# Attention and two-expert routing in one Trainium2 kernel: product banks kept from attention, the last batch's gate logits planned in attention, a third staging buffer

## The chip, the cores and the metric

One core of one Trainium2 chip runs the whole program in one launch. The metric is the device time of that launch in microseconds (us), taken on the chip. The kernel before has a median of 739.53 us over three runs (738.2 to 739.78). Five engines work side by side: PE (matrix products; its weight loads are listed as PEld), DVE and ACT (elementwise work), POOL (elementwise work and indirect transfers), and SP, whose queue only issues transfers.

## The reference, cut to what matters

Attention with 4 sink columns and a window of 128, then a mixture of 8 experts with the two best experts of each row:

```
q, k, v: (4 batches, 8 heads, 768 rows, 64)        # x: 3072 rows of 512
scores = where(sink | in_window, q @ k.T / 8, -1e9)
a = softmax(scores);  x = a @ v                    # heads side by side
noisy = x @ w_gate + log1p(exp(x @ w_noise)) * noise
top2 = the two best experts of a row; weights = softmax over the two
out[row] = sum over its two experts of weight * (relu(x @ w1[e]) @ w2[e])
```

## The kernel before, in words

The program has two parts, and each is first recorded and then laid out by a planner (class `Plan`). Every operation is recorded with its engine, a duration, a priority and what it reads and writes; `Plan.run` then lists the operations engine by engine, taking the ready one with the smallest priority, and issues the instructions in that order. Engines work their lists strictly in order, so the planner's durations and latencies decide only the order, through what counts as ready. The priorities come from the tables `PR`, `BY` and `P2`, which are the same before and after.

The first part is attention (`attention`). Its unit is a block n of 256 query rows of a pair of heads; a batch has 4 pairs of 3 blocks, so there are 48 blocks. A block has a score side: two products into the score banks `S` (L400), the previous window copied by ACT (`prev`, L404), the current window copied under a mask by DVE (`cur`, L409 and L411), the row maximum on DVE (`mins`, L421), the subtraction on POOL (`sub`), the exponential on ACT (`exps`), and for two blocks at once the row sums on DVE (`sums`, L431, and their reciprocal, L442). Up to 6 blocks may be in flight on that side (ring `C`). Behind it lies the value side: transposes of the probabilities into bank `P` (L463), copied by ACT (`CT`) and masked (`CM`); a small transpose (`pct`, L458) whose copy feeds the sink products (`sinks`, L501); the products with the values into a bank `X` (`pv`, L485 and L488); ACT's copy of the result into `turned` (L510); two transposes back (`rows`, L515); and the scaled result into `strip`, from where it is stored to `x_rows` in DRAM.

When all four pairs of a batch are there, `logits` makes the gate logits of 256 rows: products with the gate weights (`proj`, L710), ACT's copy, two transposes (`turn`, L718), and on DVE a scaling and a sum (`scale`, `total`). `routing` turns a batch's logits into places: the two best experts, the ranks (L824 to L830), and the product that puts each row number into its slot, here called the place product (`place`, L911, from the operands `rt_op` and `rt_tc`). Batches 0 to 2 are routed inside the first part. The first four tiles of 128 rows of expert 0 come from them alone: they are gathered by POOL (L1015), transposed by PE (L1099) and split by ACT and DVE into a high and a low part in `xe` (L1108 and L304).

The second part begins with these four tiles: products into the banks `H` (L1318 to L1320) and `Y` (L1350 to L1352). The last batch's logits and its routing are recorded in this part and lie between those products. Then the rows of experts 1 to 7 are gathered by POOL into a staging buffer `sg` (L1030), stored sorted to DRAM and loaded again (`xg`), and each expert's products follow (L1455 to L1457 and L1486). An output tile is scaled by ACT (L1359) into one of three `y` buffers and added into the output by POOL (L1374).

PSUM has eight banks. Attention uses four for `S`, one for `P` and three for `X`; the second part opens its own pool and takes two for `H`, one for `X`, one for `TX` and four for `Y`.

Of the kernel before, what the change touches and what calls it, by code (L numbers as in the profile page):

```python
# [75 lines left out]
SWITCH = {1: .06, 2: .05}  # L76


class Plan:
# [62 lines left out]
    def dma(self, prio, fn, us, r=(), w=(), u=(), n=1, late=0):  # L142
        self.count["dma"] = d = self.count.get("dma", -1) + 1
        self.op("SP", .48 * n, prio, fn, r, list(w) + [("dma", d)], u, lat=.65)
        self.op("DMA", us, prio, None, list(r) + [("dma", d)], w, u, lat=.95 + late)

    def run(self, dry=False):
# [21 lines left out]
        for _ in range(n):  # L169
# [26 lines left out]
            for s in succ[i]:  # L196
# [3 lines left out]
                if lat is None:  # L200
                    lat = (0 if e == "PE" else .06) if e == self.ops[s][0] else self.LAT.get((e, self.ops[s][0]), .2)
# [105 lines left out]
def attention(tc, plan, consts, cst, sh, qk_t, v, vsink, xbuf):  # L307
# [7 lines left out]
                      CT=2, CM=2, ps=2, xr=3, S=2, P=PB, X=XB, xtn=5, lt=1, lm=1, lg=2)  # L315
# [223 lines left out]
    def pair(m):  # L539
# [8 lines left out]
        op("PE", .27, n + .6 + P(g, "sinks"), lambda: sinks(m), r=[("ps", m), ("vr", (n - 1) // NJ // HP), ("vr", g // HP)], w=both, kind=3)  # L548

    def behind(n):  # L550
# [7 lines left out]
        op("ACT" if by else "DVE", .56 if by else .34, n + .7 + P(g, "rows_c"), lambda n=n, f=rows_by if by else rows_c: f(n),  # L558
# [17 lines left out]
    for g in range(NP):  # L576
        p0 = g * NJ
        e = p0 - NJ
        if g:
            load(g, None, ((g - 3) * NJ + PR.get("load_qk", 0) if g > 1 else -1980) + BY.get("load_qk", ZERO)[g])  # L580
            loads_v(g)
        else:
            plan.dma(-1997, lambda: load_v(0), 1.9, w=[("vn", 0)])
        if g % HP == 0:
            b, z = g // HP, (g - HP) * NJ if g else -6
            plan.dma((z if g else -1996.5) + BY.get("load_st", ZERO)[g], lambda b=b: sink_values(b), 2.2, w=[("st", vst[b])])
# [7 lines left out]
        for jj in range(NJ):  # L594
# [23 lines left out]
            op("PE", .44, n + .5 + P(g, "ptr"), lambda n=n: ptr(n), r=[("C", n)], w=[("P", n + NJ)], lat=(0, .21))  # L618
# [76 lines left out]
def logits(nc, plan, cst, sh, b, jj, z):  # L695
# [4 lines left out]
    last = b == sh.B - 1  # L700
    tag = "TX" if last and jj % 2 else "X"
# [23 lines left out]
    def total():  # L725
        nc.vector.tensor_reduce(get("lg", b, [128, NT, 2 * E])[:, 2 * jj:2 * jj + 2, :],
                                get(*mk).rearrange("p t h e -> p t e h"), op=OP.add, axis=AX.X)

    region = [("old", 0)] if last else []
# [7 lines left out]
def routing(nc, plan, cst, sh, b, t0, nt, z, xbuf):  # L737
# [72 lines left out]
    dve(topi, ["no", "mx"], ["ix"], .125 * nt)  # L810
# [60 lines left out]
    if not last:  # L871
        dve(lambda: v.tensor_scalar(rt("pp", pair, I32), rt("g"), 127, None, op0=OP.bitwise_and), ["g"], ["pp"], .08)
    dve(lambda: v.tensor_scalar(rt("tq", pair, I32), rt("g"), 7, None, op0=OP.logical_shift_right), ["g"], ["tq"], .08)
    if last:
        dve(lambda: v.scalar_tensor_tensor(rt("pp", pair), rt("tq"), -128.0, rt("g"), op0=OP.mult, op1=OP.add), ["g", "tq"], ["pp"], .08)
# [3 lines left out]
    def rows_of(k):  # L879
        o = rt(f"op{k}", [128, nt, 128], F16)  # L880
        for i in range(nt):
            v.tensor_scalar(o[:, i, :], c["io"], rt("pp")[:, k, i:i + 1], None, op0=OP.is_equal)

    def cols_of(k):
        o = rt(f"tc{k}", [128, nt, E * TE], F16)
        for i in range(nt):
            v.tensor_scalar(o[:, i, :], c["io1"], rt("tv")[:, k, i:i + 1], c["tok"][:, T0 + i:T0 + i + 1], op0=OP.is_equal, op1=OP.mult)

    wide = [128, nt, E * TE]
    for k in range(2) if not last else ():  # L890
# [115 lines left out]
def gather(plan, nc, cst, sh, xbuf, e, t, z, after=None):  # L1006
# [16 lines left out]
    rows, sg = cst["xsort"][m], ("sg", m + 5)  # L1023
# [22 lines left out]
    plan.op("Pool", P2["gather"], zs, sort, r=[("rt_idi", sh.B - 1)] + held, w=[sg], lat=P2["lands"])  # L1046
    plan.dma(zs, store, 1.6, r=[sg], w=[("xs", n)], late=P2["late"])
    plan.dma(z, load, 1.4, r=[("xs", n)], w=[row], late=2)
# [78 lines left out]
def w_chunk(plan, nc, cst, sh, w1, w2, e, m, i, z, lo_eng="DVE", first=()):  # L1127
# [27 lines left out]
    plan.dma(z, load, 2.2, r=list(first) + ([("at", e)] if e else []), w=[("st", n)], late=P2["late"] if e else 0)  # L1155
# [53 lines left out]
def rows_seven(plan, nc, sh, e, group, z):  # L1209
# [40 lines left out]
    split(0, 2, lambda: raw(0))  # L1250
    sums(lambda: extra(0, 2), lambda: raw(1, 2, 4), lambda: raw(1, 0, 2))
# [39 lines left out]
def experts(tc, plan, cst, sh, w1, w2, xbuf, out):  # L1291
# [9 lines left out]
    plan.rings.update(w1=4, w2a=2, w2b=2, x7=1, hb=1, ws=2, wc=2, wx=2, pick=2, raw=2, old=1, u=3, ext=2, h=FC + 1, y=3, H=2, Y=4, TX=1)  # L1301
# [9 lines left out]
    def up(q, f, i):  # L1311
        e, tiles, width = info[q]
        p = get("H", FC * q + f, [128, width], F32, "ps", [128, 512])
        both = halves(plan, sh, q)
        w = first_w(plan, f // 2).rearrange("p (x k f) -> p x k f", x=2, k=4)
        w = w[:, :, :, f % 2 * 128:(f % 2 + 1) * 128]
        xh, xl = (x[:, i, :width] for x in both)
        nc.tensor.matmul(p, w[:, 0, i], xh, start=(i == 0), stop=False)  # L1318
        nc.tensor.matmul(p, w[:, 0, i], xl, start=False, stop=False)
        nc.tensor.matmul(p, w[:, 1, i], xh, start=False, stop=(i == DC - 1))  # L1320

# [63 lines left out]
    def ends(e, t, n, z):  # L1385
# [8 lines left out]
        op("Pool", 2.65, z, lambda: scatter(e, t), r=[("y", n), ix] + [("zero", i) for i in zeros], w=[("o", n)], lat=3)  # L1394

    z = 0
    for q, (e, tiles, width) in enumerate(info):
# [14 lines left out]
        for f in range(FC):  # L1412
            k = FC * q + f
            zu = z + f * dz
            for i in range(DC):
                op("PE", (UP1 * width + .19) / DC, zu, lambda q=q, f=f, i=i: up(q, f, i),
                   r=[(x, e, t) for x in ("xh", "xl") for t in tiles] + [("w1", f // 2)], w=[("H", k)],
# [83 lines left out]
    for e in range(1, E):  # L1501
# [8 lines left out]
        for g, group in enumerate(groups):  # L1510
            for t in group:
                gather(plan, nc, c, sh, xbuf, e, t, z0 + P2["ga"] + P2["gs"] * t, begun(e, t))
                weight(plan, nc, c, sh, e, t, z0 + P2["wt"] + 3 * t)
            rows_seven(plan, nc, sh, e, group, z0 + P2["x"] + P2["xs"] * g)
# [131 lines left out]
def phase_one(tc, nc, plan, ac, tail, cst, sh, qk_t, v, vsink, w1, w2, xbuf, out):  # L1646
# [19 lines left out]
    for n in attention(tc, plan, ac, cst, sh, qk_t, v, vsink, xbuf):  # L1666
# [4 lines left out]
        if g % HP == HP - 1 and g < (sh.B - 1) * HP:  # L1671
            soon.append((n + 1, g // HP, jj))
    for t in range(sh.FA):
# [12 lines left out]

def lay_out(plan, sh, turned, of_pair, strip):
# [16 lines left out]
def carried(plan, sh):  # L1704
    n = sh.H // 2 * sh.S // 256
    return [(kx, plan.wrote[kx][-1]) for kx in (("xt", i) for i in range((sh.B - 1) * n, sh.B * n))]


def phase_two(tc, nc, plan, cst, sh, w1, w2, xbuf, out):
# [14 lines left out]
    for jj in range(NT // 2):  # L1724
        logits(nc, plan, cst, sh, b, jj, -200)
# [78 lines left out]
```

## Time and profile before

| what | us |
|---|---|
| median of three runs | 739.53 |
| profiled execution | 739.88 |
| its span, first to last instruction | 738.3 |
| PE busy | 700.4 (95%) |
| DVE busy | 546.5 (74%) |
| ACT busy | 409.1 (55%) |
| POOL busy | 324.5 (44%) |

The span is 1.58 us shorter than the execution it comes from. Shares of busy time are averages over stages that are limited by different engines, so the table alone does not say what a change is worth; the rows further down are taken by stage.

### The profile page before, as it was taken

To read this page: it belongs to the slowest core of one execution; us is meant where nothing else is said; L and a number is where in the kernel's file an instruction comes from. 1 tells how busy PE (TensorE), PEld (TensorE's weight loads), DVE (VectorE), ACT (ScalarE), POOL (GpSimd) and SP (SyncE) were. 2 spreads that over 40 slices of the span, in tenths; PEclk is the share of its full clock that TensorE was granted. 3 is DMA by queue.
4 is the path that set the end of the run, shared out by engine and by line. 5 is a ranking of instruction groups with operands and counts; after the bars stand their busy time and mean duration, and the time that the engine had idled before them with its cause. 6 is when DMAs were issued, how large, how long until landed. Compare 5 with 4: busy or idle time off the path is not lost.

```text
span 738.3 us, 13436 instructions
## 1 busy us (share of the span) xinstructions
PE 700.4 (95%) x4731; PEld 587.1 (80%) x4731; DVE 546.5 (74%) x1300; ACT 409.1 (55%) x924; POOL 324.5 (44%) x431
## 2 busy tenths in 40 slices
PE   5999998998999999998999999999999999999995
PEld 3666666666768989888888998899889889889984
DVE  6699999986753898694878678676877878775710
ACT  3877788685222465554664456455555546555520
POOL 4567698795332552283226223431632440080022
PEclk9999999999999999999999999999999999999998
DMA  8565786646267998767747663857485393263133
GB/s 302 149 201 156 219 266 185 214 124 187 69 203 223 239 274 255 220 150 172 210 121 183 164 190 83 210 156 206 93 227 174 94 214 104 87 115 86 58 44 44
DMA packets 87320, 123.13 MB, mean 167 GB/s; under 512 B 18641, under 2 KB 55377, under 8 KB 87249
## 3 DMA queue, kind: packets, MB, share of 16 engines
q1 hardware_dynamic: 75856, 94.64, 41.8%
q0 software_dynamic: 11392, 27.60, 19.6%
q8 instruction: 38, 0.62, 0.4%
q14 instruction: 34, 0.27, 0.1%
HBM read 81.49 MB, written 40.73 MB: 166 GB/s over the span
## 4 chain that ended last, share of the span: by engine, by line
PE 73%; DVE 9%; ACT 7%; DMA 6%; issue 2%; POOL 1%; SPq 0%; POOLq 0%; ACTq 0%; DVEq 0%
PE Y L1486 28%; PE H L1455 5%; PE H L1456 5%; PE H L1457 5%; PE X L1455 3%; PE X L1457 3%; PE X L1456 3%; PE S L400 2%; ACT strip L521 2%; DMA st<-in_w2c 2%; PE P L463 2%; DMA out<-tmp,idx 2%; PE Y L1489 2%; PE X L485 1%; PE H L1318 1%
## 5 line engine op out<-in xcount | busy, mean ns | idle before, releaser
L1374 POOL DMA_INDIRECT out<-tmp,idx x34 | 80.5, 2367 | 157.0 <-ACT tmp L1359 149.0
L1486 PE MATMUL Y<-w2a,hb 128*128 128x512 f32 x504 | 129.5, 396 | 0.0
L1486 PE MATMUL Y<-w2b,hb 128*128 128x512 f32 x504 | 124.5, 391 | 0.0
L1486 PEld LDWEIGHTS Y<-w2b,hb 128*128 128x128 f32 x504 | 94.5, 188 | 19.8
L1486 PEld LDWEIGHTS Y<-w2a,hb 128*128 128x128 f32 x504 | 94.5, 188 | 19.4
L1456 PE MATMUL H<-x,wr 128*128 128x384 f32 (+1 forms) x224 | 77.1, 344 | 0.3 <-DVE x L304 0.3
L1030 POOL DMA_INDIRECT sg<-x_rows,rt_idi x45 | 48.6, 1080 | 54.6 <-DMA x_sorted<-sg 32.1
L304 DVE TENSOR_TENSOR wr<-st,wr 128x512 fp32r<-128x512 f32 (+1 forms) x86 | 59.7, 697 | 9.0 <-ACT wr L1185 8.3
L1185 ACT ACTIVATE wr<-st 128x512 fp32r<-128x512 f32 x84 | 52.3, 625 | 17.7 <-DVE st L304 17.2
L1455 PE MATMUL H<-xe,wr 128*128 128x384 f32 (+1 forms) x168 | 58.2, 347 | 2.5 <-ACT tmp L1470 1.7
L304 POOL TENSOR_TENSOR cbuf<-cbuf,mn 128x528 f32<-128x528 f32 x48 | 52.5, 1096 | 11.9 <-DVE mn L421 7.3
L1457 PE MATMUL H<-xe,wr 128*128 128x384 f32 (+1 forms) x168 | 57.6, 343 | 0.0
L400 PE MATMUL S<-kq 64*64 64x196 f32 (+1 forms) x768 | 48.4, 354 | 7.7 <-DVE cbuf L411 5.0
L1374 POOL DMA_INDIRECT out<-turned,idx x18 | 36.2, 2012 | 36.5 <-ACT turned L1359 30.2
L1045 POOL COPY spacer<-hb 1x1 f32<-1x1 f32 x38 | 12.0, 315 | 89.0 <-ACT hb L1476 81.8
L1359 ACT ACTIVATE tmp<-Y,wc 128x512 f32<-128x512 f32 x31 | 21.3, 688 | 50.4 <-PE Y L1486 28.9
L1470 ACT ACTIVATE tmp<-H 128x384 f32<-128x384 f32 (+1 forms) x56 | 28.0, 500 | 34.1 <-PE H L1457 31.0
L1456 PEld LDWEIGHTS H<-x,wr 128*128 128x128 f32 x224 | 42.1, 188 | 2.8 <-DVE x L304 0.6
L411 DVE COPY_PREDICATED cbuf<-le,S 128x256 f32<-128x256 uint8 x80 | 33.8, 442 | 12.1 <-ACT cbuf L404 11.7
L400 PEld LDWEIGHTS S<-kq 64*64 64x64 f32 x768 | 22.6, 138 | 24.0 <-DVE cbuf L411 12.6
L304 DVE TENSOR_TENSOR w2a<-st,w2a 128x1024 fp32r<-128x1024 f32 x16 | 19.6, 1223 | 27.3 <-ACT w2a L1144 27.3
L1455 PE MATMUL X<-x,wr 128*128 128x384 f32 (+1 forms) x112 | 38.7, 345 | 1.1 <-ACT x L1241 1.1
(335 smaller groups left out, 1809.7 us busy)
## 6 DMA issues: line engine op xcount, KB each, us to landing
st<-in_w1c SPq DMA_DIRECT2D x32, 512.0 KB
st<-in_w2c SPq DMA_DIRECT2D x32, 512.0 KB
x_sorted<-sg SPq DMA_DIRECT2D x45, 272.0 KB
kq<-in_qk_t SPq DMA_DIRECT2D x15, 780.0 KB
xg<-x_sorted SPq DMA_DIRECT2D x42, 272.0 KB
out<-zt SPq DMA_DIRECT2D x31, 256.0 KB
vn<-in_v SPq DMA_DIRECT2D x16, 384.0 KB
x_rows<-strip SPq DMA_DIRECT2D x48, 128.0 KB
```

Of the source, the lines that this page charges most:

```text
L304: eng.tensor_tensor(out, a, b, op=OP.subtract)
L400: nc.tensor.matmul(whole[x, h, c0:c1], kq(g)[r, KS + 128 * j + 64 * s:KS + 128 * j + 64 * s + 64], kq(g)[r, o + c0:o + c1], start=True, st ...
L411: nc.vector.copy_predicated(c, le[:, None, :].to_broadcast([128, 2, 128]), p)
L1030: nc.gpsimd.indirect_dma_start(out=stage(), out_offset=None, in_=xbuf, in_offset=bass.IndirectOffsetOnAxis(ap=cst["idw"]()[:, sh.TE * e + ...
L1185: plan.op("ACT", .03 + .255 * m, z, lambda: nc.scalar.activation(h(), src(), AF.Copy), r=[st], w=[(*key, b)] + old, u=[key, ex], lat=P2["s ...
L1359: nc.scalar.activation(get("y", Y[e, t], [128, DM]), get("Y", Y[e, t]), AF.Copy, scale=c["wc"][e % 2][:, t:t + 1])
L1374: d = nc.gpsimd.indirect_dma_start(out=out, out_offset=bass.IndirectOffsetOnAxis(ap=c["idx"][:size(e, t), e, t:t + 1], axis=0), in_=get("y ...
L1455: nc.tensor.matmul(p, wh, h, start=start and not k, stop=False, skip_group_check=True)
L1456: nc.tensor.matmul(p, wh, l, start=False, stop=False, skip_group_check=True)
L1457: nc.tensor.matmul(p, wl, h, start=False, stop=k == 1, skip_group_check=True)
L1470: nc.scalar.activation(u_of(e, k), src(), AF.Copy)
L1486: nc.tensor.matmul(p, h[:, x * (CAP + R) + 128 * t:x * (CAP + R) + 128 * t + 128], w[:, y], start=(f == 0 and x + y == 0), stop=(f == FC - ...
```

## The change: what it does

1. The four banks of `P` and `X` are now four tiles `B0` to `B3` that outlive attention. In the second part `H`, `X` and `TX` are views of them; the pool of the second part holds `Y` alone.
2. The last batch's logits are recorded in the first part, each 256 rows after their last attention block, as for the other batches. The second part starts with the routing of that batch.
3. Sorted rows are staged in three buffers: every third tile goes to the end of `xe`, behind the split rows of the seven experts. The first use waits until the products that read `xe` whole are done.
4. The operands of the last batch's place product are made by whole-tile operations, as for the other batches, and not row by row.
5. The rows of expert 1 get other priorities.
6. The planner's costs change (same-engine latencies on DVE and ACT, changes of tile shape on PE, transfers). They cost nothing themselves, but move instructions.

```
-SWITCH = {1: .06, 2: .05}
+SWITCH = {1: .105, 2: .09}
+SELF = {"PE": 0, "DVE": .14, "ACT": .15}
...
-        self.op("DMA", us, prio, None, list(r) + [("dma", d)], w, u, lat=.95 + late)
+        self.op("DMA", us, prio, None, list(r) + [("dma", d)], w, u, lat=1.2 + (.6 if us > .7 else 0) + late)
...
-                    lat = (0 if e == "PE" else .06) if e == self.ops[s][0] else self.LAT.get((e, self.ops[s][0]), .2)
+                    lat = SELF.get(e, .06) if e == self.ops[s][0] else self.LAT.get((e, self.ops[s][0]), .2)
...
-    last = b == sh.B - 1
-    tag = "TX" if last and jj % 2 else "X"
+    tag = "X"
...
-    for k in range(2) if not last else ():
+    for k in range(2):
...
-    for k in range(2) if last else ():
-        dve(lambda k=k: rows_of(k), ["pp"], [f"op{k}"], .1 * nt, kind=PORT)
-        dve(lambda k=k: cols_of(k), ["tv"], [f"tc{k}"], .085 * nt, kind=PORT)
...
-    rows, sg = cst["xsort"][m], ("sg", m + 5)
+    rows = cst["xsort"][m]
+    sg = ("sx", m // 3) if m % 3 == 2 else ("sg", 5 + m // 3 * 2 + m % 3)
...
-    plan.op("Pool", P2["gather"], zs, sort, r=[("rt_idi", sh.B - 1)] + held, w=[sg], lat=P2["lands"])
+    plan.op("Pool", P2["gather"], zs, sort, r=[("rt_idi", sh.B - 1)] + held + [("xe", f) for f in range(sh.F // 128)] * (m == 2), w=[sg], lat=P2["lands"])
...
-            rows_seven(plan, nc, sh, e, group, z0 + P2["x"] + P2["xs"] * g)
+            rows_seven(plan, nc, sh, e, group, z0 + P2["x"] + (P2["xs"] if e > 1 else 5) * g, 20 if e == 1 else 0)
...
-            logits(nc, plan, cst, sh, b, jj, n + PR.get("lg", .5))
-            if jj == NJ - 1:
+            logits(nc, plan, cst, sh, b, jj, n + PR.get("lg" if b < sh.B - 1 else "ll", .5))
+            if jj == NJ - 1 and b < sh.B - 1:
...
-        if g % HP == HP - 1 and g < (sh.B - 1) * HP:
+        if g % HP == HP - 1:
...
+def banks(*regions):
+    held = {}
+
+    def get(i, shape, dt):
+        if shape is not None:
+            held[i] = view(regions[i % len(regions)], 0, shape, dt)
+        return held[i]
+
+    return get
...
-    for jj in range(NT // 2):
-        logits(nc, plan, cst, sh, b, jj, -200)
...
+            flat = both.enter_context(tc.tile_pool(name="flat", bufs=1, space=bass.MemoryType.PSUM))
+            bank = [flat.tile([128, 512], F32, name=f"B{i}") for i in range(4)]
...
+            plan.laid.update(P=banks(bank[0]), X=banks(*bank[1:]), xtn=of_pair, xr=lambda n, shape, dt: view(strip, n % 3 * 256, [128, 2, 2, sh.D], F32))
...
+        k = (plan.count["X"] + 1) % 3
+        near = [bank[1 + (k + i) % 3] for i in range(3)]
+        p2.laid.update(H=banks(near[0], bank[0]), X=banks(near[1]), TX=banks(near[2]))
```

DVE's list near the end of attention, before, from the last operand of batch 2's place product (`rt_tc1`) on; `cbuf` holds the score side, `mn` its maxima, `sm` its sums, and `idg` is the list by which expert 0's first rows are gathered:

```order
L895 TENSOR_TENSOR rt_tc1_2775<-io1_85,rt_tv_2754 128x336
L409 TENSOR_TENSOR cbuf_163<-S0_74,m0_160 128x2x128
L411 COPY_PREDICATED cbuf_163<-le_156,S1_75 128x2x128
L421 TENSOR_REDUCE mn_2800<-cbuf_163 128x4
L411 COPY_PREDICATED cbuf_163<-le_156,S0_74 128x2x128
L421 TENSOR_REDUCE mn_2833<-cbuf_163 128x4
L926 SCALAR_TENSOR_TENSOR idg_134<-X_2820,ga_111 128x4
L928 TENSOR_TENSOR idx_135<-X_2820,sa_112 128x4
L953 TENSOR_TENSOR ids_107<-ids_107,X_2820 128x56
L411 COPY_PREDICATED cbuf_163<-le_156,S0_74 128x2x128
L421 TENSOR_REDUCE mn_2861<-cbuf_163 128x4
L431 TENSOR_REDUCE sm_2875<-cbuf_163 128x8
```

The same place in the changed kernel's DVE list:

```order
L882 TENSOR_TENSOR rt_tc1_2753<-io1_92,rt_tv_2713 128x336
L432 TENSOR_REDUCE sm_2756<-cbuf_170 128x8
L443 RECIPROCAL ri_2191<-sm_2756 128x4x2
L525 TENSOR_TENSOR strip_151<-B1_75,ri_2191 128x256
L910 SCALAR_TENSOR_TENSOR idg_141<-B3_77,ga_118 128x4
L912 TENSOR_TENSOR idx_142<-B3_77,sa_119 128x4
L937 TENSOR_TENSOR ids_114<-ids_114,B3_77 128x56
L525 TENSOR_TENSOR strip_151<-B2_76,ri_2191 128x256
```

All masked copies and maxima of the score side now stand ahead of the place product's operands; behind them, one sum is left of two.

PE's list where attention ends and the first expert's products begin, before (`xe` are the four split tiles, `wr` the weights; `sg` and `xg` the gathered rows):

```order
L485 MATMUL X_2964<-CT_2979,vn_2857 64x128 x4
L488 MATMUL X_2964<-CM_2969,dv_2934 64x128 x4
L515 MATMUL X_2936<-idf_66,turned_143 128x128 x2
L1099 MATMUL X_3002<-idf_66,sg_2901 128x128 x4
L515 MATMUL X_2964<-idf_66,turned_143 128x128 x2
L1099 MATMUL X_3012<-idf_66,sg_2932 128x128 x4
L1099 MATMUL X_3021<-idf_66,xg_2961 128x128 x4
L1099 MATMUL X_3030<-idf_66,xg_2983 128x128 x4
L710 MATMUL X_3056<-turned_143,wbd_80 32x256 x4
L710 MATMUL TX_3061<-turned_143,wbd_80 32x256 x4
L1318 MATMUL H_3067<-xe_3010,wr_1588 128x512
```

And in the changed kernel:

```order
L489 MATMUL B1_75<-CM_2862,dv_2840 64x128 x4
L516 MATMUL B3_77<-idf_66,turned_150 128x128 x2
L710 MATMUL B2_76<-turned_150,wbd_87 32x256 x4
L516 MATMUL B1_75<-idf_66,turned_150 128x128 x2
L710 MATMUL B3_77<-turned_150,wbd_87 32x256 x4
L718 MATMUL B2_76<-idf_66,lt_2918 128x128 x2
L1093 MATMUL B1_75<-idf_66,sg_2811 128x128 x4
L718 MATMUL B3_77<-idf_66,lt_2935 128x128 x2
L1093 MATMUL B2_76<-idf_66,sg_2828 128x128 x4
L1093 MATMUL B1_75<-idf_66,xg_2857 128x128 x4
L1093 MATMUL B3_77<-idf_66,xg_2833 128x128 x4
L1066 MATMUL B2_76<-xe_2939,wr_1418 128x512
```

The logits' products and transposes (L710, L718) now stand among the last attention rows and the row tiles, and none is left among the expert's products.

## Rows read from the trace of the kernel before

**Rows 1.** The page: busy time, share of the span and instructions of each engine.

```profile
PE 700.4 (95%) x4731; PEld 587.1 (80%) x4731; DVE 546.5 (74%) x1300; ACT 409.1 (55%) x924; POOL 324.5 (44%) x431
```

**Rows 2.** Busy time by stretch: length, each engine, then granted clock, DMA share, GB/s.

```profile
10.00:60.00 50.00, 44.75 (x540) 31.26 (x536) 40.81 (x74) 37.95 (x109) 30.39 (x46) 0.97 0.61 196
60.00:163.00 103.00, 94.73 (x1304) 65.98 (x1303) 97.66 (x260) 83.52 (x253) 84.72 (x142) 1.00 0.70 203
183.00:214.00 31.00, 29.17 (x177) 21.80 (x178) 21.90 (x102) 8.28 (x15) 10.38 (x14) 1.00 0.43 129
214.00:331.00 117.00, 116.64 (x573) 102.18 (x572) 87.17 (x209) 56.33 (x112) 53.09 (x58) 1.00 0.81 224
331.00:353.00 22.00, 18.33 (x90) 16.36 (x89) 11.82 (x30) 9.79 (x20) 9.19 (x11) 1.00 0.75 174
353.00:704.00 351.00, 350.27 (x1725) 315.05 (x1724) 266.73 (x574) 192.81 (x370) 108.81 (x109) 1.00 0.56 145
```

**Rows 3.** DVE, 162 to 184 us, in order of time: start, us, what, idle before.

```profile
162.56 0.92 DVE L895 TENSOR_TENSOR rt_tc<-io,rt_tv 128x336 f16<-128x336 f16 x2
...
165.98 0.45 DVE L411 COPY_PREDICATED cbuf<-le,S 128x256 f32<-128x256 uint8 x1 [1.23 <-ACT cbuf L404]
166.46 0.70 DVE L421 TENSOR_REDUCE mn<-cbuf 128x4 f32<-128x528 f32 x1
...
168.65 1.25 DVE L431 TENSOR_REDUCE sm<-cbuf 128x8 f32<-128x1064 f32 x1
...
170.15 0.20 DVE L442 RECIPROCAL ri<-sm 128x8 f32<-128x8 f32 x1
...
181.68 1.34 DVE L304 TENSOR_TENSOR xe<-X,xe 128x512 fp32r<-128x512 f32 x2
```

**Rows 4.** PE, 164 to 191 us, in order of time.

```profile
165.39 0.61 PE L911 MATMUL X<-rt_tc,rt_op 128*128 128x56 f16 x12
...
170.52 0.44 PE L501 MATMUL X<-ps,vr 64*128 64x128 f32 x4
170.89 0.66 PE L485 MATMUL X<-CT,vn 128*64 128x128 f32 x8
171.38 0.61 PE L488 MATMUL X<-CM,dv 128*64 128x128 f32 x8
171.91 0.66 PE L463 MATMUL P<-idf,cbuf 128*128 128x128 f32 x4
...
172.68 0.44 PE L515 MATMUL X<-idf,turned 128*128 128x128 f32 x2
...
181.03 0.63 PE L1099 MATMUL X<-idf,xg 128*128 128x128 f32 x4 [0.25 <-DMA xg<-x_rows,idg]
183.07 0.64 PE L710 MATMUL X<-turned,wbd 128*32 128x256 f32 x8 [1.41 <-DVE xe L304]
...
184.88 0.38 PE L718 MATMUL X<-idf,turned 128*128 128x128 f32 x2
```

**Rows 5.** What PE waited for, 183 to 330 us: total us, times, longest.

```profile
PE TX L1099 <- DMA sg<-x_rows,idg: 0.9, 1, 0.9
PE X L824 <- DVE m L816: 0.4, 1, 0.4
PE X L948 <- DVE x L943: 0.4, 1, 0.4
```

**Rows 6.** Waits, 305 to 362 us, the rows of the output path.

```profile
ACT tmp L1359 <- DMA out<-tmp,idx: 8.6, 2, 6.8
...
POOL sg L1030 <- DMA x_sorted<-sg: 5.8, 2, 3.5
```

**Rows 7.** Stretches in which PE is little busy, columns as in rows 2.

```profile
24.00:26.00 2.00, 1.26 (x21) 0.83 (x20) 1.46 (x5) 2.00 (x6) 1.35 (x3) 1.00 0.80 162
...
28.00:30.00 2.00, 2.00 (x18) 1.11 (x15) 1.23 (x3) 1.25 (x4) 1.47 (x3) 0.50 0.60 188
...
178.00:184.00 6.00, 3.46 (x34) 2.03 (x32) 3.71 (x10) 2.78 (x6) 0.06 (x1) 1.00 0.82 192
```

More of the change, by code (lines that the diff above doesn't have):

```diff
@@ L870, in routing @@
         ["ix", "r2"], ["g"], .08)
-    if not last:
-        dve(lambda: v.tensor_scalar(rt("pp", pair, I32), rt("g"), 127, None, op0=OP.bitwise_and), ["g"], ["pp"], .08)
+    dve(lambda: v.tensor_scalar(rt("pp", pair, I32), rt("g"), 127, None, op0=OP.bitwise_and), ["g"], ["pp"], .08)
     dve(lambda: v.tensor_scalar(rt("tq", pair, I32), rt("g"), 7, None, op0=OP.logical_shift_right), ["g"], ["tq"], .08)
-    if last:
-        dve(lambda: v.scalar_tensor_tensor(rt("pp", pair), rt("tq"), -128.0, rt("g"), op0=OP.mult, op1=OP.add), ["g", "tq"], ["pp"], .08)
     dve(lambda: v.tensor_scalar(rt("vl", pair), rt("r2"), float(sh.CAP), None, op0=OP.is_lt), ["r2"], ["vl"], .08)
@@ L1074, in rows_region, with up_part @@
     return plan.get("hb", 0, [128, 8 * (2 * CAP + 64)], F32R, "sb")
+def up_part(plan, nc, sh, q, f, i, width, p):
+    w = first_w(plan, f // 2).rearrange("p (x k f) -> p x k f", x=2, k=4)[:, :, :, f % 2 * 128:(f % 2 + 1) * 128]
+    xh, xl = (x[:, i, :width] for x in halves(plan, sh, q))
+    nc.tensor.matmul(p, w[:, 0, i], xh, start=(i == 0), stop=False)
+    nc.tensor.matmul(p, w[:, 0, i], xl, start=False, stop=False)
+    nc.tensor.matmul(p, w[:, 1, i], xh, start=False, stop=(i == sh.DM // 128 - 1))
 def first_w(plan, i):
@@ L1154, in w_chunk @@
         plan.op("SP", .3, z - .01, which, r=[("eid", 0)], w=[("at", e)])
-    plan.dma(z, load, 2.2, r=list(first) + ([("at", e)] if e else []), w=[("st", n)], late=P2["late"] if e else 0)
+    plan.dma(z, load, 1.35, r=list(first) + ([("at", e)] if e else []), w=[("st", n)], late=P2["late"] if e else 0)
     if e and m == 1:
@@ L1250, in rows_seven @@
     split(0, 2, lambda: raw(0))
+    z += more
     sums(lambda: extra(0, 2), lambda: raw(1, 2, 4), lambda: raw(1, 0, 2))
@@ L1311, in up @@
     def up(q, f, i):
[L1312 to L1320, printed above, removed]
+        up_part(plan, nc, sh, q, f, i, info[q][2], get("H", FC * q + f, [128, info[q][2]], F32, "ps", [128, 512]))
     def cut(q):
@@ L1416, in experts @@
                 op("PE", (UP1 * width + .19) / DC, zu, lambda q=q, f=f, i=i: up(q, f, i),
-                   r=[(x, e, t) for x in ("xh", "xl") for t in tiles] + [("w1", f // 2)], w=[("H", k)],
+                   r=[(x, e, t) for x in ("xh", "xl") for t in tiles] + [("w1", f // 2)], w=[("H", k)] + [("xe", f)] * (not q),
                    u=region + [("wr", f // 2), ("hb", 0)])
@@ L1704, in carried @@
 def carried(plan, sh):
-    n = sh.H // 2 * sh.S // 256
-    return [(kx, plan.wrote[kx][-1]) for kx in (("xt", i) for i in range((sh.B - 1) * n, sh.B * n))]
+    return [(kx, plan.wrote[kx][-1]) for kx in [("lgs", (sh.B - 1) * sh.S // 256 + i) for i in range(sh.S // 256)]]
 def phase_two(tc, nc, plan, cst, sh, w1, w2, xbuf, out):
```

56 lines of the change are left out of this document (25 added, 31 removed).

## The prediction, made before the changed kernel ran

> **What bounds the kernel now.** I read four views in this order. First the stretches: PE is busy 116.64 of 117 us from 214 to 331 and 350.27 of 351 from 353 to 704, so with its 95% [rows 1, 2] the second part is a solid row of products. A delay of the first of them passes undiminished to the end. Only two places there are loose: 183 to 214 us, with 1.83 us idle, and 331 to 353, with 3.67 [rows 2]. Second, the same view for attention: from 60 to 163 us DVE is busy 97.66 of 103 us and PE 94.73 [rows 2]; from 10 to 60 DVE has 40.81 of 50. So DVE carries attention, with 9.19 + 5.34 = 14.5 us idle between 10 and 163. Third, the instructions where attention ends: batch 2's place product lies at 165.39 to 166.00, and everything of expert 0's start hangs on it: indices, gather, transposes on PE, splits on DVE. PE is let go by the last split at 183.07, runs two `proj` of the logits, and starts the first expert product at 184.07 [rows 3, 4]. Fourth, the waits of the second part [rows 5, 6].
>
> So the time is: the moment of the place product, plus 18.07 us to the first expert product, plus a nearly solid rest.
>
> **The change, term by term.** All sums are made on the profiled execution, 739.88 us (738.3 of span and 1.58 around it); the median of the runs is 0.35 lower, which I take off at the end.
>
> 1. *DVE ahead of the place product.* The order shows that after the change all masked copies and maxima stand ahead of the operand `rt_tc1`. Compared line by line over the whole of DVE's list up to there, that is four more current-window copies (I price the one L409 among them as an L411), three more maxima, one more sum and one more reciprocal: 4 x 0.45 + 3 x 0.70 + 1.25 + 0.20 = 5.35, taken as 5.3 us [rows 3]. Either they push the place product back by all of it, or they fill idle time that DVE had. With 14.5 us idle in 153, and the planner's costs for DVE now larger, so that it lists fewer steps behind one they depend on, about half should be filled: 2.5 us. Net +2.8. Bounds: nothing filled, +5.3; 8 us filled, a little over half of the idle time, -2.7. This is the least certain term, since an order shows no idle time.
>
> 2. *From the place product to the first expert product.* Before, 18.07 us. Behind the place product only four blocks remain after the change, not six, but the logits' work joins them. PE's share by rows: two sink products 2 x 0.44; four value products, each pair of L485 and L488 some 1.10 (170.89 to 171.99), 4.4; four row transposes 4 x 0.44, 1.76; two transposes into `P`, 2 x 0.66, 1.32; three `proj` at 0.5 (two fill 183.07 to 184.07), 1.5; three `turn` at 0.38, 1.14; four row tiles at 0.63, 2.5. Sum 13.5 us [rows 4]. The chain isn't gapless: results go PE to ACT to PE, PE to DVE to PE, some six times, and a step like the last wait of PE, 1.41 us, or the 0.25 for the gather, stands for each; at 0.7 that is 4.5. Then the last split of a pair, 1.34 [rows 3], with ACT's high part ahead of it, some 0.6: 20 us in all, against 18.07: +1.9. Bounds: 15.5 if the waits are only the last two (13.5 + 1.34 + some 0.6), which is -2.6; 21.5 if each wait is 1 us, +3.4.
>  The same place shows what is moved: on DVE the logits' scaling and sum now lie between the splits of the row tiles, on a queue that works strictly in order, so a late `turn` holds a split and the first product behind it. Before, they lay behind the splits.
>
> 3. *Logits among the products.* Before, the third `proj` and three `turn` sat between the products: 0.5 + 3 x 0.38 = 1.64 by adding [rows 4]. Matrix products overlap at their ends, so less than that goes; I take 1.2, with 0.8 and 1.64 as bounds. Saved: -1.2.
>
> 4. *Routing of the last batch.* Its logits are ready some microseconds earlier relative to the products, and its operands are made whole-tile, as the 0.92 us of L895 in batch 2 [rows 3], not row by row. PE waited 0.9 + 0.4 + 0.4 = 1.7 us in this stretch [rows 5]. I take 1.2 of these as saved; bounds -1.7 and 0. The gather wait of 0.9 can stay, as the list behind it still has to pass POOL and a transfer. Taken: -1.2.
>
> 5. *Expert 1.* In 331 to 353 us PE idles 3.67 [rows 2]; beside it ACT waited once 6.8 us for an output transfer and POOL up to 3.5 us for a sorted store [rows 6]. The third staging buffer takes that POOL wait away, and the sorted gather no longer lies among expert 1's output transfers in POOL's list. But ACT's wait is for a transfer out of a `y` buffer, and that is untouched. Taken: -0.5. Bounds: the whole gap, -3.7; or, where the third buffer's first gather, which now waits for all products that read `xe`, holds the gathers behind it, +3.
>
> 6. *At nothing.* The four PSUM banks add no instruction; their cover is that `H`, `X` and `TX` are views of banks whose last readers in attention end before the products start. Without it one reader, a row transpose's scaled copy, would hold the first product for one of the six waits of term 2, 0.7 us. The planner's costs take no time themselves; what they move is in terms 1 and 2. The ring `lg` of one serves three batches in turn, each read by routing long before the next is written, so it is hidden; a wait there would stand on DVE's `total`, and cost the same 0.7.
>
> Sum: 739.88 + 2.8 + 1.9 - 1.2 - 1.2 - 0.5 = 741.7; on the scale of the median 741.3.
>
> **The clock, weighed apart.** PE was busy 1.26 of 2 us from 24 to 26, and its granted clock stood at 0.50 from 28 to 30, the lower of the two levels, 1.2 GHz: 2 us there did the work of one. But from 178 to 184 PE was busy 3.46 of 6 and the clock stayed at 1.00 [rows 7]. So sparse stretches here can cost the clock or not, and the end of attention has kept it so far. The Trainium skill, "TensorE: Matmul & The Clock Gate", section "HAM oscillation — how this bites in real kernels", says that a stream of products which stalls between bursts is put back to half clock, and that each burst then starts cold. By that rule a thinner tail of attention would take time beyond term 2; the row at 24 us agrees with it, the row at 178 us doesn't. By the row alone, nothing is added; by the rule, at least the 1.0 us that the row at 28 us lost.
>
> **The rivals.**
> *A. The attention itself gets shorter.* If DVE's idle time is filled by 8 us and not by 2.5, term 1 becomes -2.7 and the sum 736.2, or 735.8 as a median. It ends on the faster side from 4.3 us filled on (741.7 less 1.8 is 739.9). For it: 9.19 us of idle lie in 10 to 60 us, where DVE is no bound at all and where an order with truer latencies has most to give. Against it: from 60 to 163 us it is at 95% already.
> *B. Expert 1 starts late.* The sorted gather into the end of `xe` holds POOL's list for the 3.5 us that its longest wait for a buffer had [rows 6], in place of -0.5: 741.7 + 4 = 745.7, 745.3 as a median. For it: one more condition on a queue in order. Against it: the products that read `xe` end long before experts 1 to 7 are wanted, and PE has no idle in 214 to 331.
> *C. The change doesn't do what it says.* The logits leave one full stretch of PE for another, and what attention gains it gives back at the place product: terms cancel, 739.5.
> *D. The clock falls in the thinner tail.* One or two such stretches of 2 us at half clock before the first product, at 1.0 us lost in each [rows 7]: 742.3 to 743.3.
>
> **How the numbers follow.** A difference of 0.2%, 1.5 us, is about what a measurement of this kernel can tell from no change: faster is below 738.05, slower above 741.0. The forecast has 0.42: its own range is 739.5 to 744, of which 0.31 lies above 741.0 and 0.11 within. A has 0.32, 0.30 of it faster and 0.02 within. B has 0.09 and D 0.05, all slower. C has 0.12: 0.05 faster, 0.06 within, 0.01 slower. Faster 0.35, same 0.19, slower 0.46. The range goes from 734.5, where A has filled some 9 us, to 747, where B comes on top of +1.7 from the other terms.
>
> **What would show it.** Term 1: the end of the place product, 166.0 before; I expect 168.8, A expects 163 or less. And DVE's idle time from 10 us to that product, about 12 against some 6. Term 2: from the end of the place product to the first expert product, 20 us. Term 3: no `proj` or `turn` among the products. Term 4: the waits of 1.7 us behind the first products down to some 0.5. Term 5: PE's idle time around the end of expert 0, 3.2 us; under B over 6, with POOL's wait for the row buffer in the stretch before. D: a granted clock below 1.00 in the 15 us before the first product. The forecast is wrong if the first expert product starts before 186 us, which needs either the place product earlier or the tail shorter.

## The result, and the profile after

The changed kernel takes 747.42 us (745.87 to 749.59, 4 runs) against 738.87 before (737.43 to 739.78, 4 runs). The ratio is 1.012 with a 95% interval of 1.0088 to 1.0151: slower by 8.6 us (1.2%). The forecast was 741.3, with a range up to 747. The profiled execution is the shortest of the four, 745.87 us, with a span of 744.2.

The busy time of each engine has hardly moved:

```profile
PE 704.3 (95%) x4731; PEld 588.0 (79%) x4731; DVE 548.4 (74%) x1282; ACT 409.9 (55%) x924; POOL 314.4 (42%) x431
```

The stretches of the changed kernel, with the columns and the bounds of [rows 2]:

```profile
10.00:60.00 50.00, 46.13 (x574) 31.24 (x574) 43.42 (x80) 38.93 (x113) 33.16 (x50) 1.00 0.65 218
60.00:163.00 103.00, 91.43 (x1187) 62.76 (x1186) 92.08 (x222) 79.18 (x233) 76.88 (x125) 0.93 0.61 182
183.00:214.00 31.00, 28.58 (x209) 21.56 (x210) 21.97 (x85) 10.92 (x22) 8.81 (x14) 1.00 0.46 131
214.00:331.00 117.00, 112.81 (x554) 97.75 (x553) 78.63 (x191) 52.32 (x105) 43.04 (x55) 1.00 0.78 225
331.00:353.00 22.00, 22.00 (x104) 19.17 (x103) 18.63 (x49) 10.97 (x25) 13.26 (x13) 1.00 0.89 191
353.00:704.00 351.00, 350.35 (x1727) 315.33 (x1726) 270.40 (x577) 193.60 (x372) 108.40 (x111) 1.00 0.56 148
```

Against [rows 2], 10 to 60 us has become better: DVE is busy 43.42 us and not 40.81. But from 60 to 163, DVE falls from 97.66 to 92.08, and the mean granted clock to 0.93. In the second part PE's gap at 331 to 353 is gone, and 4.19 us of idle time stand ahead of it, from 214 to 331, where there was 0.36.

Two instructions of PE give the sum: the place product of batch 2, and the first product of the experts. In the kernel before they are at 165.39 [rows 4] and here:

```profile
184.07 0.50 PE L1318 MATMUL H<-xe,wr 128*128 128x512 f32 x1
```

In the changed kernel:

```profile
177.04 0.47 PE L895 MATMUL B<-rt_tc,rt_op 128*128 128x56 f16 x12
...
193.74 0.50 PE L1066 MATMUL B<-xe,wr 128*128 128x512 f32 x1 [0.74 <-ACT xe L1102]
```

The place product ends at 177.51, 11.5 us later than the 166.0 of [rows 4]. From there to the first product it is 16.23 us and not 18.07: 1.84 less. From the first product to the end of the span it is 550.46 (744.2 - 193.74) and not 554.23 (738.3 - 184.07): 3.77 less. 11.5 - 1.84 - 3.77 = 5.9, the difference of the spans. So everything that was lost lies ahead of the place product. Up to there, from 10 us on, DVE (the third engine column) has done more work and has also been idle longer; the kernel before and then the changed one:

```profile
10.00:166.00 156.00, 142.34 (x1875) 99.30 (x1871) 140.24 (x337) 124.47 (x373) 118.12 (x194) 0.99 0.67 198
10.00:177.51 167.51, 150.35 (x1919) 103.60 (x1919) 147.99 (x345) 129.45 (x383) 123.09 (x200) 0.96 0.61 188
```

DVE's work is 7.75 us more (147.99 against 140.24), its idle time 3.76 us more (19.52 against 15.76); together they are the 11.5.

Where most of it arose, is seen from the finished blocks. ACT copies each block's result into `turned`; the 18th and the 19th copy stand so, in the kernel before:

```profile
81.32 0.37 ACT L510 ACTIVATE turned<-X 128x256 f32<-128x256 f32 x1
85.88 0.38 ACT L510 ACTIVATE turned<-X 128x256 f32<-128x256 f32 x1 [0.24 <-PE X L488]
```

and in the changed one:

```profile
76.07 0.38 ACT L511 ACTIVATE turned<-B 128x256 f32<-128x256 f32 x1
92.68 0.36 ACT L511 ACTIVATE turned<-B 128x256 f32<-128x256 f32 x1
```

The changed kernel is 5.3 us ahead after 18 blocks, and 6.8 behind after 19: it loses 12 us at one place. At the 36th block, the last of batch 2, it is still 6.7 us behind (149.91 against 143.20). The other 4.8 us come between that block and the place product: 27.60 us against 22.80, in which 8 more blocks are finished and not 6. The place of the 12 us in steps of 2 us (columns as in [rows 2]):

```profile
82.00:84.00 2.00, 0.55 (x9) 0.35 (x9) 2.00 (x6) 1.40 (x5) 2.00 (x3) 1.00 0.91 294
84.00:86.00 2.00, 1.02 (x24) 0.51 (x16) 2.00 (x6) 1.50 (x5) 1.25 (x3) 0.67 0.93 358
86.00:88.00 2.00, 2.00 (x24) 1.12 (x16) 2.00 (x4) 1.31 (x3) 1.12 (x2) 0.50 1.08 375
88.00:90.00 2.00, 0.10 (x2) 0.00 (x0) 2.00 (x4) 0.09 (x1) 0.54 (x2) 0.50 0.91 353
90.00:92.00 2.00, 1.45 (x14) 1.45 (x16) 0.50 (x1) 0.82 (x1) 1.42 (x1) 0.50 0.39 149
92.00:94.00 2.00, 1.86 (x14) 1.26 (x11) 0.12 (x1) 1.80 (x5) 1.68 (x1) 0.50 0.04 18
94.00:96.00 2.00, 2.00 (x16) 1.47 (x14) 1.08 (x4) 0.88 (x2) 1.72 (x4) 0.77 0.22 66
```

DVE works without a break to 90 us, while PE starves; then PE runs at half clock, and DVE has nothing to do. What DVE did and what PE wanted, in order of time:

```profile
87.02 0.82 DVE L305 TENSOR_TENSOR dv<-vn 128x640 f32<-128x640 f32 x1
87.75 0.21 DVE L443 RECIPROCAL ri<-sm 128x8 f32<-128x8 f32 x1
87.87 1.22 DVE L432 TENSOR_REDUCE sm<-cbuf 128x8 f32<-128x1064 f32 x1
89.01 0.69 DVE L422 TENSOR_REDUCE mn<-cbuf 128x4 f32<-128x528 f32 x1
89.62 0.20 DVE L443 RECIPROCAL ri<-sm 128x8 f32<-128x8 f32 x1
89.73 0.77 DVE L305 TENSOR_TENSOR dv<-vn 128x640 f32<-128x640 f32 x1
93.88 0.42 DVE L525 TENSOR_TENSOR strip<-B,ri 128x256 f32<-128x256 f32 x1 [3.38 <-ACT turned L511]
```
```profile
86.98 1.12 PE L486 MATMUL B<-CT,vn 128*64 128x128 f32 x8
90.55 0.69 PE L489 MATMUL B<-CM,dv 128*64 128x128 f32 x4 [2.45 <-DVE dv L305]
```

PE holds the value product of head pair 6 and waits for that pair's `dv`, the difference of its values. The DVE list names the tiles: the `dv` at 87.02 is pair 7's, which nobody needs yet, and pair 6's, for which PE waits, comes last, at 89.73, though its values were loaded 11 us earlier than pair 7's. Ahead of this wait PE had waited 1.5 us for POOL and 1.4 us for DVE's masked copies, from 81 to 86 us. Behind PE's waiting product lie the score products, so DVE, too, soon starves. The table of single-pair priorities adds 29.29 to that of pair 6's `dv`: it comes when nothing with a smaller priority is ready. With the same number and the old costs (a_oldcosts, below) the two `dv` run at 80.34 and 88.87, and PE waits for neither.

In the same place ACT waited 3.1 us for a weight transfer. The chain that ended last goes through it, and it names another culprit:

```profile
82.34 8.82 DMA st<-in_w1c
91.16 0.02 issue
91.18 1.06 ACT wr L1138
```

### The profile page after: what moved, and what is told of

Its sections match the earlier page's. It is cut to its first block, busy times and chain, and to the rows that moved or that the text cites. A ratio compares the mean times of both kernels' runs of the same rounds, so it can differ in the third digit from the quotient of the medians.

```text
span 744.2 us, 13428 instructions
## 1 busy us (share of the span) xinstructions
PE 704.3 (95%) x4731; PEld 588.0 (79%) x4731; DVE 548.4 (74%) x1282; ACT 409.9 (55%) x924; POOL 314.4 (42%) x431
## 3 DMA queue, kind: packets, MB, share of 16 engines
q0 software_dynamic: 11392, 27.60, 19.0%
## 4 chain that ended last, share of the span: by engine, by line
PE 71%; DVE 12%; DMA 7%; ACT 4%; POOL 3%; issue 2%; SPq 0%; POOLq 0%; ACTq 0%; DVEq 0%
PE Y L1473 28%; PE B L1442 9%; PE B L1443 9%; PE B L1444 9%; DMA xg<-x_sorted 4%; PE S L401 3%; PE B L486 2%; PE B L464 2%; PE B L489 2%; PE Y L1476 1%; DMA sg<-x_rows,idg 1%; DVE x L305 1%; DMA st<-in_w1c 1%; DVE mn L422 1%; PE B L1067 1%
## 5 line engine op out<-in xcount | busy, mean ns | idle before, releaser
L1443 PE MATMUL B<-x,wr 128*128 128x384 f32 (+1 forms) x392 | 134.9, 344 | 1.4 <-DVE x L305 1.4
L1443 PEld LDWEIGHTS B<-x,wr 128*128 128x128 f32 x392 | 73.6, 188 | 4.8 <-DVE x L305 2.1
L1444 PE MATMUL B<-xe,wr 128*128 128x384 f32 (+1 forms) x224 | 76.8, 343 | 0.0
L1442 PE MATMUL B<-xe,wr 128*128 128x384 f32 (+1 forms) x224 | 76.8, 343 | 0.0
L305 POOL TENSOR_TENSOR cbuf<-cbuf,mn 128x528 f32<-128x528 f32 x48 | 53.9, 1125 | 21.5 <-DVE mn L422 14.6
L1442 PE MATMUL B<-x,wr 128*128 128x384 f32 (+1 forms) x168 | 58.1, 346 | 1.2 <-DVE tmp L1460 0.7
L1444 PE MATMUL B<-x,wr 128*128 128x384 f32 (+1 forms) x168 | 57.6, 343 | 0.0
L401 PE MATMUL S<-kq 64*64 64x196 f32 (+1 forms) x768 | 50.7, 366 | 5.9 <-DVE cbuf L412 2.7
L1457 ACT ACTIVATE tmp<-B 128x384 f32<-128x384 f32 (+1 forms) x56 | 28.0, 500 | 40.5 <-PE B L1444 36.5
L1361 POOL DMA_INDIRECT out<-turned,idx x18 | 31.8, 1766 | 39.8 <-ACT turned L1346 36.5
L1442 PEld LDWEIGHTS B<-xe,wr 128*128 128x128 f32 x224 | 42.1, 188 | 2.1
L1015 POOL DMA_INDIRECT sg<-x_rows,rt_idi x30 | 31.1, 1036 | 27.2 <-DMA x_sorted<-sg 12.6
L1444 PEld LDWEIGHTS B<-xe,wr 128*128 128x128 f32 x224 | 42.0, 188 | 0.2
```

What stands on the lines that cost most here:

```text
L305: eng.tensor_tensor(out, a, b, op=OP.subtract)
L401: nc.tensor.matmul(whole[x, h, c0:c1], kq(g)[r, KS + 128 * j + 64 * s:KS + 128 * j + 64 * s + 64], kq(g)[r, o + c0:o + c1], start=True, st ...
L1015: nc.gpsimd.indirect_dma_start(out=stage(), out_offset=None, in_=xbuf, in_offset=bass.IndirectOffsetOnAxis(ap=cst["idw"]()[:, sh.TE * e + ...
L1361: d = nc.gpsimd.indirect_dma_start(out=out, out_offset=bass.IndirectOffsetOnAxis(ap=c["idx"][:size(e, t), e, t:t + 1], axis=0), in_=get("y ...
L1442: nc.tensor.matmul(p, wh, h, start=start and not k, stop=False, skip_group_check=True)
L1443: nc.tensor.matmul(p, wh, l, start=False, stop=False, skip_group_check=True)
```

## The experiments

In all kernels below the computation is whole. Ratios are against the kernel before, run beside them. Edits that only set planner's numbers add and remove no instruction.

**Costs or structure.** One kernel is the one before with the planner's new costs, the other the changed one with the old costs.

```
b_costs:     before + SWITCH, SELF, dma(...), durations of operations and transfers, scatter
a_oldcosts:  after  - the same
```

> The kernel before with the planner's new costs alone (SWITCH, SELF, transfers, operation durations, scatter); no instruction is added or removed. Theory A (the costs reorder attention badly: pair 7's value difference dv is listed on DVE ahead of pair 6's, as in the changed kernel): the place product of batch 2 moves from 166 us to 173 or later, a granted clock below 1.00 stands around 80 to 100 us, and the time is 744 to 750. Theory B (the loss comes from the structure: logits in attention and the banks): same as before within 1.5 us, 737.5 to 740.5.

> The changed kernel with the planner's old costs; the banks, the logits in attention, the third staging buffer, the whole-tile operands and expert 1's priorities stay. Theory A: no stall of PE at pair 6, place product at 164 to 168 us, the gain of some 3.8 us behind the first expert product stays, so 734 to 738. Theory B: 745 to 749 as the changed kernel.

b_costs: 754.66 us, ratio 1.0179 (1.0142 to 1.0217), above theory A's 744 to 750 but with its signs: the place product at 178.2, and this in place of 19.90 us of DVE and a clock of 1.00:

```profile
80.00:100.00 20.00, 15.00 (x156) 10.47 (x156) 14.62 (x28) 11.34 (x30) 13.42 (x19) 0.66 0.56 180
```

a_oldcosts: 736.36, ratio 0.9948 (0.9921 to 0.9975), and 735.41, 0.9956 (0.9932 to 0.998) when run again:

> The changed kernel with the planner's old costs once more, beside the others on one chip: 735 to 738, ratio 0.993 to 0.998.

Its rows from 80 us, of the second part, and of PE:

```profile
80.00:100.00 20.00, 18.35 (x277) 13.54 (x269) 19.90 (x46) 16.43 (x45) 15.06 (x22) 1.00 0.84 253
214.00:331.00 117.00, 114.42 (x562) 99.86 (x561) 84.26 (x202) 56.17 (x113) 48.65 (x58) 1.00 0.80 222
331.00:353.00 22.00, 21.36 (x108) 19.80 (x107) 16.16 (x44) 11.82 (x25) 9.26 (x11) 1.00 0.84 215
```
```profile
164.87 0.32 PE L894 MATMUL B<-rt_tc,rt_op 128*128 128x56 f16 x6 [0.20 <-POOL rt_tc L884]
185.57 0.50 PE L1065 MATMUL B<-xe,wr 128*128 128x512 f32 x1 [0.69 <-ACT xe L1101]
```

Theory B falls, and of A it holds that the costs make the loss: points 1 to 5 of the change gain 0.5% as long as the costs stay old, and the costs alone, which add not one instruction, lose 1.8% even in the kernel before.

**The one late `dv`, or ACT's wait.**

```
- dv=(..., -0.16, 29.29, -0.59, ...)
+ dv=(..., -0.16, 0, -0.59, ...)
```

> The changed kernel with one number changed: the priority added to the value difference dv of pair 6 is 0, not 29.29; everything else as changed. Theory A1 (that one late instruction on DVE starves PE from 81 to 91 us, and the halved clock follows): PE's wait of 2.5 us for dv is gone, the granted clock stays 1.00 there, and some 5 to 8 us come back: 739 to 743. Rival A2 (ACT's wait of 3.1 us for a weight transfer at 88 us is what stops the blocks): the time stays at 745 or more, with ACT's wait still there.

749.30 us, ratio 1.0119 (1.0087 to 1.0151): the time did not come back, so A1 is wrong as a forecast. At its place it was right. Pair 6's `dv` runs at 84.61, PE doesn't wait for it, the 19th block is finished at 86.6 and not at 93.0, and the clock holds. And the weight transfer, issued at 82.81, took 7.2 us to land (8.8 in the changed kernel), but ACT's conversion of it does not wait, since ACT has blocks to work on until then:

```profile
91.20 0.38 ACT L405 ACTIVATE cbuf<-S 128x264 f32<-128x264 f32 x1
91.47 1.05 ACT L1138 ACTIVATE wr<-st 128x1024 fp32r<-128x1024 f32 x1
```

So ACT's wait, on which the chain had put the place, was for the most part idle time of an engine that lacked work; what it cost by itself is at most the 1.4 us by which the conversion and the operation behind it held the 19th copy (its products ended at 91.24, it started at 92.68). But the kernel then stalls in batch 2, with a place product waiting on PE for DVE:

```profile
80.00:100.00 20.00, 16.28 (x233) 11.21 (x229) 18.16 (x38) 14.12 (x36) 14.80 (x21) 1.00 0.83 265
120.00:140.00 20.00, 14.80 (x180) 10.93 (x179) 16.87 (x45) 11.52 (x33) 14.07 (x22) 0.85 0.69 191
140.00:165.00 25.00, 21.62 (x253) 13.31 (x253) 21.44 (x44) 16.19 (x44) 13.80 (x20) 0.92 0.25 81
```

At the 32nd block it is still with the kernel before (127.8 against 128.7 us); the 36th is finished at 153.4 against 143.2. So the late `dv` was one bad place in an order that has others. In the changed kernel itself PE is short of work once more, from 128 to 132 us (2.46 us busy of 4), and the clock falls again behind it:

```profile
132.00:136.00 4.00, 4.00 (x48) 2.62 (x50) 3.48 (x9) 2.04 (x5) 1.92 (x4) 0.57 0.74 184
```

**Which costs.**

```
a_nodma:   after, transfers at their old durations and latency
a_noself:  after, old SWITCH and no SELF
```

The durations of the other operations and the sorted rows' extra latency stay new in both.

> The changed kernel with the planner's old costs for transfers alone (their durations and latency); SELF, SWITCH and the rest stay new. Theory S (the latencies of DVE and ACT and the tile-shape changes of PE do the harm): 744 to 750, with a stall of PE and a clock below 1.00 in attention. Theory D (the transfers that are believed to land earlier do it): no such stall, 735 to 739. If any change of costs does harm, because priorities fit the old ones only: both this and its counterpart above 740.

> The changed kernel with the old SWITCH and without SELF (DVE's and ACT's own latencies at 0.06, PE's tile changes at 0.06 and 0.05); the costs of transfers and the rest stay new. Theory S: no stall, 735 to 739. Theory D: 744 to 750. If any change of costs does harm: above 740 in both.

745.86 us, ratio 1.0091 (1.006 to 1.0122), and 758.29, ratio 1.0263 (1.0224 to 1.0302). Neither of these two groups of costs is the culprit alone: with either of them old, the kernel is about as slow as with all costs new, or slower.

**The fit of the priorities.** If any change of costs does harm, the suspect is what was kept: the table `BY`, which shifts single pairs. It was set to 0 under the new and under the old costs, and under the new ones in the structure of before.

```
+ BY = {k: ZERO for k in BY}
```

> The changed kernel (new costs) with every priority of the table BY, which shifts single pairs of heads, set to 0; PR and P2 stay. Theory M (the single-pair priorities fit the old costs only, so under the new ones they are noise or worse): no slower than the changed kernel's 747 by more than 4 us, and within 4 us of its counterpart with old costs. Theory C (the new costs themselves lay the work out worse, whatever the priorities): 6 us or more above the counterpart with old costs.

> The changed kernel with the planner's old costs and every priority of the table BY set to 0. Theory M: the 736 us under old costs rest on that table, so 743 to 755, and within 4 us of the counterpart with new costs. Theory C: 6 us or more below the counterpart with new costs.

> The kernel before with the planner's new costs and the table BY at zero; its structure is that of before. If the table under the new costs is all that made b_costs (754.7) slow: 735 to 742. If the new costs suit only the changed structure: 748 or more.

| | old costs, table | new costs, table | old costs, no table | new costs, no table |
|---|---|---|---|---|
| structure before | 1 | 1.0179 | not run | 0.9997 (0.9981 to 1.0012) |
| structure after | 0.9948, 0.9956 | 1.012 | 1.012 (1.0093 to 1.0147) | 0.9949 (0.9927 to 0.9972) |

In microseconds the lower row is 736.4 and 735.4, 747.4, 746.8, 735.8. By the ratios the table is worth some 1.7%, 12 us, under the old costs, and costs as much under the new ones. Of theory M the first half held, better than it said; its second half, equal times without the table, did not: without it the new costs are 11 us better than the old ones, the reverse of theory C. So the new costs do no harm by themselves: the loss needs them and the table together, and the change renewed one of the two. With the table out, the structure's gain under the new costs is again 0.5% (0.9949 against 0.9997). Why the old costs without the table are slow isn't shown. That the table was fitted to the old costs is inferred from the times; four settings do not exclude that two of the orders merely happen to be good. The table `PR` stayed as it was in all of them. In n_flat the place product ends at 167.33, DVE is busy 19.27 of 20 us from 80 to 100, and the clock there is 1.00:

```profile
166.71 0.62 PE L896 MATMUL B<-rt_tc,rt_op 128*128 128x56 f16 x12
187.74 0.50 PE L1067 MATMUL B<-xe,wr 128*128 128x512 f32 x1 [0.74 <-ACT xe L1103]
```
```profile
80.00:100.00 20.00, 19.68 (x258) 12.78 (x258) 19.27 (x39) 16.42 (x42) 16.23 (x22) 1.00 0.85 286
165.00:185.00 20.00, 17.29 (x162) 12.09 (x163) 8.74 (x23) 6.52 (x16) 9.02 (x12) 0.83 0.48 143
```

**What the structure's 0.5% is made of.** All with the planner's old costs, each without one part.

```
o_nosx:     sg = ("sg", m + 5)                     # two staging buffers
o_exp1:     expert 1's rows and weights at their old priorities
o_neither:  both
o_rowops:   the last batch's place operands row by row
```

> The changed kernel with the planner's old costs (736.4 measured, ratio 0.995) and without the third staging buffer: sorted rows use the two sg buffers alone. If the third buffer carries the gain of the second part: the gap of PE around the end of expert 0 comes back, 2 to 4 us longer, 738.5 to 740.5. If the logits and the operands carry it: no change, 736 to 737.5.

> The changed kernel with the planner's old costs and the old priorities of expert 1's rows and weights. If expert 1's priorities carry the gain at 331 to 353 us: PE's gap there is back to 3 to 4 us, 738.5 to 740.5. If they do nothing under these costs: 736 to 737.5.

> The changed kernel with the planner's old costs, without the third staging buffer and with expert 1's old priorities; the banks, the logits in attention and the whole-tile operands stay. If the gain is the logits' and the operands': still below before, 735.5 to 738. If the buffer and the priorities carry it between them: no gain over before, 738.5 to 741.

> The changed kernel with the planner's old costs and the last batch's place operands made row by row, as before the change. If the whole-tile operands bring forward the last batch's places: PE waits 0.5 to 1.2 us more among the first products, 737 to 738. If they hide behind products either way: 736 to 736.8.

736.29 (0.9981, 0.9956 to 1.0006), 737.56 (0.9978, 0.9957 to 0.9999), 737.29 (0.9974, 0.9952 to 0.9995) and 737.64 us (0.9986, 0.9967 to 1.0005). By their ratios all four lie above the two runs with all parts, by 0.2 to 0.4%, but the intervals overlap: what each is worth stays open. That o_neither is still below before leaves the logits, banks and operands a part of it. PE's gap at 331 to 353 came back in none at its full size: it was 0 without the third buffer and 1.23 us without the priorities. But the place had moved: without the third buffer PE is idle for 3.78 us from 255 to 275, 2.02 with it.

**The second part's costs, and a better version.** The first has old costs in attention (its order there is that of a_oldcosts, word for word) and new ones in the second part; the second the reverse, with `BY` at 0.

> The changed kernel with the planner's old costs while attention is planned and its new costs while the second part is planned; attention's order is that of the old costs, word for word. If the new costs do their harm in attention alone: 734 to 738, as with old costs in both. If they also harm the second part: 1 to 4 us above that, with PE idle between 214 and 331 us as in the changed kernel (4.2 us there). If they help the second part: below 735.

> The changed kernel with the table BY at zero, attention planned with the new costs and the second part with the old ones. If the old costs suit the second part better (735.4 against 737.7 with attention under old costs): 733 to 735.5. If the second part under new costs is as good: 735.5 to 737.5.

737.73 us, 0.9984 (0.9962 to 1.0006), and 734.34 us, 0.9964 (0.9942 to 0.9986). With attention under old costs, old ones in the second part are ahead of new ones by 0.3% (0.9948 and 0.9956 against 0.9984); with attention under new costs and no table they aren't (0.9964 against n_flat's 0.9949). All intervals overlap, so the second part's costs stay open; what they do is small beside attention's order. flat_old2, n_flat and a_oldcosts are all below both kernels; which of the three is best, these runs can't tell.

## Why the prediction was wrong

The sign was forecast; the size was not, and the time lay above the range.

*Term 1 failed.* It said +2.8 us, with -2.7 and +5.3 as bounds; measured were +11.5. It added 5.3 us of DVE's work and took off 2.5, because larger costs should let the order fill idle time. The work was counted rightly: four copies, three maxima, one sum and one reciprocal more do stand ahead of the operand. DVE's busy time up to the product grew by 7.75 us, and where the other 2.4 lie isn't shown. The filling was the wrong step: DVE's idle time up to the place product did not fall by 2.5 us, it grew by 3.76, and the bound "nothing filled" supposed that the rest of the order is as good as before. It wasn't: pair 7's `dv` stands ahead of pair 6's and PE behind it, and in 80 to 100 us DVE's busy time fell from 19.90 (before, and in a_oldcosts) to 13.56 us. That the planner's costs "take no time themselves; what they move is in terms 1 and 2" is the sentence that hid it. The prediction went through DVE's whole list, but counted in it what stands ahead of one operand and did not look for neighbours that had changed places.

In n_flat the term comes out almost as it was reasoned:

```profile
10.00:167.33 157.33, 144.37 (x1911) 99.31 (x1905) 145.83 (x342) 128.21 (x381) 120.64 (x199) 0.99 0.66 202
```

DVE's work there is 5.59 us more than before, its idle time 4.26 us less (11.50 against 15.76), and the place product ends 1.33 us later. So the filling is possible in this structure; the order that was planned with the new costs and the old table did not have it.

*Term 2* said 20 us from place product to first product, bounds 15.5 and 21.5; it was 16.23. (Its own parts give 19.6: six waits at 0.7 are 4.2, not 4.5.) Four blocks were left, as it supposed. PE's work was right, 12.94 us against the 13.5 that it added up; too large were the waits and the last split, 3.29 us where it had 6.5. a_oldcosts has 20.38 (165.19 to 185.57) and n_flat 20.41, but with six and five blocks left, so they don't confirm it.

*Terms 3 to 5* said -2.9 together; from the first product to the end it is 3.77 us less. That the sum came near is partly luck, as PE's share in that stretch shows, before and after:

```profile
184.07:738.28 554.21, 538.83 (x2657) 475.38 (x2653) 389.12 (x912) 271.57 (x524) 190.99 (x201) 1.00 0.60 156
193.74:744.20 550.46, 536.09 (x2639) 473.81 (x2639) 386.65 (x891) 270.20 (x521) 181.35 (x201) 1.00 0.59 156
```

Term 3 (no `proj` or `turn` is left among the products) said -1.2, and PE's work fell by 2.74 us. Terms 4 and 5 said -1.7, and PE's idle time fell by 1.0. Of term 4's waits of 1.7 us [rows 5], L824's is gone and L948's (now L932) is 0.2, but that for the gathered rows grew from 0.9 to 1.4. Term 5's gap at 331 to 353 went wholly, but not the idle time: PE's idle time from 214 to 353 is 4.19 us against 4.03, and the products that waited in that gap (L1455 and L1456, now L1442 and L1443) wait 1.8 us from 273 to 284. What PE waits for in 190 to 360 now:

```profile
PE B L1093 <- DMA sg<-x_rows,idg: 1.4, 2, 1.2
PE B L1443 <- DVE x L305: 1.4, 2, 1.1
...
PE Y L1473 <- DVE hb L1466: 0.7, 1, 0.7
PE B L1442 <- DVE tmp L1460: 0.7, 1, 0.7
```

None of them is a sorted gather, so rival B's mechanism isn't what was seen.

*The rivals.* Rival A had the other sign, and its reason, that other latencies in the planner fill DVE's idle time, is what n_flat shows: 45.16 us of DVE from 10 to 60 against 40.81 before and 40.02 in o_flat. The changed kernel had some of it too, 5.3 us ahead at 76 us, before the stall took it. (On the prediction's own scale A is faster from 5.8 us filled on, not 4.3: 738.05 is 3.3 below 741.3.) *The clock*, rival D, fell, but in the middle of attention and not in its tail: behind 1.57 us of work in 4 (82 to 86 us) the granted clock was 0.50, the lower level, and it was at 1.00 again from 96. The rule of the Trainium skill, "TensorE: Matmul & The Clock Gate", section "HAM oscillation — how this bites in real kernels", says that a stream of products which stalls between bursts is put back to half clock; here the trace agrees in the direction, though that section's stream waits for DMA and this one waited for POOL and DVE. The lower clock came behind the stall and added to it: by the six rows from 84 to 96, 3.5 us of work were not done (each row's busy time by what its clock lacks of 1.00: 0.34, 1.00, 0.05, 0.73, 0.93 and 0.46), and by the row from 132 to 136 another 1.7. The prediction weighed the clock for the stretch behind the place product alone, where it stayed at 1.00.

## What to carry to other kernels

A planner's priorities and its costs have to be renewed together: changing the costs while keeping the table of priorities lost 1.8% in the kernel before, and dropping the table along with the old costs gave it all back. Whether the new costs are closer to the chip was not measured. Where a change touches what orders the work, read the whole order for instructions that changed places with a neighbour, above all an operand that another engine's list waits for, before counting work at one place. And where the chain of waits points at a transfer, ask whether the waiting engine had anything else to do.

## What the runs showed of the hardware

The same transfer of 512 KB into `st` took from 3.8 to 8.8 us to land in the changed kernel's attention (median 5.5); the 8.8 were with transfers issued on both sides of it at 81.32, 81.79, 84.77 and 85.15. In n_flat the mean granted clock was 0.83 from 165 to 185 us, in the tail where the kernel before had kept 1.00 [rows 7], and the kernel was still 11.6 us faster than the changed one.
